# Keys and x transposed on VectorE and through DRAM instead of on TensorE

## The chip, the cores and the metric

The kernel runs on one core of a Trainium2 chip. The metric is the time of one execution in device microseconds; 0.3% of it is about 1 us. TensorE, VectorE, ScalarE, GpSimd and SyncE are five engines that run their own instruction streams in order and wait for each other by semaphores. In the profile they are PE (matmuls), PEld (weight loads of TensorE), DVE, ACT, POOL and SP; SP issues nearly all DMAs here.

## The reference

The first part is linear attention with a forget gate, for batch B = 4, H = 8 heads, S = 768 steps and head size D = 48. The second takes its output as x (4 x 768 x 384) through a rotation by learned angles, a mixing over steps with two 768x768 matrices, and a channel layer.

```python
f = 1.0 / (1.0 + np.exp(-f_logit))
for t in range(S):
    state = f[:, :, t, :, None] * state + np.einsum('bhd,bhe->bhde', k[:, :, t], v[:, :, t])
    y[:, :, t] = np.einsum('bhd,bhde->bhe', q[:, :, t], state)
# x: y with the heads side by side
theta = x @ w_theta
zr, zi = x * np.cos(theta), x * np.sin(theta)
y = np.einsum('ts,bsd->btd', w_tok_r, zr) + np.einsum('ts,bsd->btd', w_tok_i, zi)
u = x + y
return u + np.maximum(u @ w_ch, 0.0)
```

## The kernel before

A chunk is 128 steps of one batch with all heads; there are 24, six per batch. q, k and f of a chunk lie as [128, 4, 128]: two heads (each padded from 48 to 64 rows) fill the 128 partitions, four pairs stand side by side, and the 128 steps run along the row. The recurrence is turned into matrix products inside a chunk: the gates' logarithms are summed along the steps ("gs"), q is scaled by the running product p ("gq"), k by its inverse ("gk").

Everything after the set-up is written as a list of short steps, ORDER. The loop at its end (L578) takes one name after another, counts how often each name has come, and emits that step's instructions for that chunk, so the n-th "sc" is chunk n-1. A name with "/A", "/D" or "/P" is put on ScalarE, VectorE or GpSimd in place of its usual engine. No planner moves anything: each engine carries out its instructions in the order of the list, and so does SyncE with its DMAs.

For the attention of one chunk: "lf", "lk", "lq", "lv" load f, k, q and v; "go", "gs", "ge", "gp" make the gates; "ke" transposes the four key pairs on TensorE into PSUM (L321) and "kt" copies them to SBUF (L146 is the copy helper's line), because the state's update needs the steps on the partitions. "sc" (L295, L301) multiplies keys by v and keys by q; "ma" masks, "sa", "st", "sm" carry the state on, "oa" (L354) and "ob" (L365) multiply with state and v, "xc" copies the result to x, with steps on the partitions.

For the second part: "xt" transposes x in three blocks on TensorE (L377); from PSUM "xs" copies it to the u tile and "xh" and "xl" split it into a rounded value and the rest. "th" (L407) multiplies nine times by w_theta for the angles, "tn", "se", "ab", "tr" reduce them and take sine and cosine, "ro" multiplies by x, "zh" and "zl" split the result. 144 pieces "f" (L461) of six matmuls (the first 18 of two in full precision, four records each) add up the mixing; a group of 18 pieces is done for a batch and half of the steps. Then "v" adds to u, "uh" and "ul" split, "c" (L479, nine matmuls) is the channel layer, "cv" adds and "so" stores. "lw" loads weights, "d2" to "d5", "e4" and "e5" decode and split them; "wu" is a warm-up matmul. "fl" reduces a flag that says whether a rarely needed general branch must follow, "rv" loads it into registers, "bh" hints that branch.

Buffers: three each of f, k and q, two of v, one of transposed keys ("ktok"), three of x, three of u, one each of the rounded x and its rest, 25 of "wp" (values, weights and the first products' inputs), four PSUM banks "a" and four "mix".

Of the kernel before, what the change touches and what calls it, by code (L numbers as in the profile page):

```python
# [21 lines left out]
DM = H * D  # L22
# [23 lines left out]
CUT = 0  # L46

# [41 lines left out]
)  # L89


@with_exitstack
def gla_moe_kernel(
    ctx: ExitStack,
    tc: tile.TileContext,
    q: bass.AP,
    k: bass.AP,
    f: bass.AP,
# [286 lines left out]
    def u_slice(m):  # L385
        return uts[m // 3][:, :, m % 3 * C:(m % 3 + 1) * C]
# [318 lines left out]
```

## Time and profile before

| | |
|---|---|
| time, three runs | 334.07, 334.29, 334.9 us (median 334.29) |
| span of the profiled execution, first to last instruction | 331.3 us (its own time is not listed apart from the runs) |
| TensorE matmuls busy | 319.2 us, 4430 records |
| VectorE busy | 247.8 us, 448 instructions |
| ScalarE busy | 197.4 us |
| GpSimd busy | 49.3 us |
| DMA moved | 43.17 MB in 21,649 packets |
| granted TensorE clock | 0.999 of 2.4 GHz |

A matmul's length contains the time in which the next one already runs, so a busy TensorE may be less than a full one; the chain of waits has the pace at which groups follow each other. Full-precision matmuls have two records each.

### The profile page before, as it was taken

The numbers are of one execution on the slowest core, as the hardware profiler recorded it, in microseconds if no ns is written. First come the engines' busy times: TensorE is split into PE (matmuls) and PEld (weight loads), VectorE is DVE, ScalarE is ACT, GpSimd is POOL, SyncE is SP. The second block draws the span as 40 slices with busy tenths as digits, with TensorE's granted clock in tenths as the row PEclk, the third lists the DMA queues.
The fourth block names the chain that finished last, engine by engine and source line by source line (L and its number), as shares of the span: only waits on it lengthen the run. The fifth ranks groups of instructions, "written<-read, shape, count | busy, mean of one in ns | idle before, by whom it ended". The sixth has DMA issues, their size and how long they took to land.

```text
span 331.3 us, 10287 instructions
## 1 busy us (share of the span) xinstructions
PE 319.2 (96%) x4430; PEld 295.2 (89%) x4430; DVE 247.8 (75%) x448; ACT 197.4 (60%) x356; POOL 49.3 (15%) x65
## 2 busy tenths in 40 slices
PE   7689999999998999999999999999999999999993
PEld 7578677669998999999999999999999999999993
DVE  3789999999998999898954686766687868533252
ACT  6789999996888888574765378435844114300000
POOL 3230123124133310012101120200010100000000
PEclk9999999999999999999999999999999999999999
DMA  7979998567543270262126134108101000000022
GB/s 227 382 239 344 325 321 313 159 207 230 184 146 101 49 256 0 67 224 82 53 83 213 34 123 156 40 2 264 48 2 39 28 24 26 0 24 26 24 72 78
DMA packets 21649, 43.17 MB, mean 130 GB/s; under 512 B 2400, under 2 KB 5472, under 8 KB 21600
## 3 DMA queue, kind: packets, MB, share of 16 engines
q1 hardware_dynamic: 21456, 42.27, 38.4%
q8 instruction: 36, 0.59, 0.7%
q10 hardware_dynamic: 144, 0.20, 0.2%
q14 instruction: 13, 0.11, 0.1%
HBM read 37.74 MB, written 4.72 MB: 128 GB/s over the span
## 4 chain that ended last, share of the span: by engine, by line
PE 86%; DVE 5%; ACT 2%; DMA 2%; issue 1%; SPq 1%; DVEq 0%; ACTq 0%
PE pm L461 44%; PE pch L479 12%; PE pth L407 11%; PE pss L365 4%; PE pss L354 4%; PE pss L295 4%; PE pss L301 3%; PE psk L321 3%; PE pxt L377 2%; DMA v<-in_v_dram 2%; SPq L524 1%; DVE k L262 1%; ACT z L146 1%; DVE f L242 1%; PE warm L316 1%
## 5 line engine op out<-in xcount | busy, mean ns | idle before, releaser
L461 PE MATMUL pm<-wp,z 128*128 128x384 f32 x756 | 144.7, 340 | 0.0
L461 PEld LDWEIGHTS pm<-wp,z 128*128 128x128 f32 x756 | 130.3, 188 | 1.1 <-DVE wp L216 0.3
L479 PE MATMUL pch<-uhl,wch 128*128 128x384 f32 x216 | 41.4, 340 | 0.0
L479 PEld LDWEIGHTS pch<-uhl,wch 128*128 128x128 f32 x216 | 37.2, 188 | 0.2
L242 DVE TENSOR_TENSOR_SCAN f<-carry,f 128x512 f32<-128x512 f32 x24 | 29.1, 1217 | 5.0 <-ACT f L238 4.8
L407 PE MATMUL pth<-wth,xh 128*128 128x384 f32 x144 | 30.1, 344 | 0.9 <-ACT x L146 0.9
L146 ACT CAST uhl<-ut 128x384 fp32r<-128x384 f32 x12 | 6.2, 516 | 38.1 <-DVE uhl L146 19.9
L493 DVE SCALAR_TENSOR_TENSOR ut<-pch,ut 128x384 f32<-128x384 f32 x24 | 13.1, 554 | 20.7 <-PE pch L479 20.6
L407 PEld LDWEIGHTS pth<-wth,xh 128*128 128x128 f32 x144 | 24.7, 188 | 1.6 <-ACT x L146 1.2
L461 PE MATMUL pm<-value,zf 128*128 128x384 f32 x72 | 26.0, 497 | 0.0
L307 DVE TENSOR_TENSOR sc<-pss,causal 128x256 f32<-128x256 f32 x48 | 18.0, 416 | 8.4 <-PE pss L354 8.4
L257 POOL TENSOR_TENSOR q<-q,p 128x512 f32<-128x512 f32 x13 | 17.2, 1323 | 40.7 <-ACT p L249 39.3
L340 POOL TENSOR_TENSOR st<-st,pes 128x192 f32<-128x192 f32 x12 | 8.7, 721 | 95.9 <-DVE st L336 95.9
L249 ACT ACTIVATE p<-f 128x512 f32<-128x512 f32 x24 | 15.1, 628 | 9.8 <-DVE f L242 9.0
L253 POOL COPY pes<-p 128x4 f32<-128x4 f32 x24 | 11.4, 475 | 62.4 <-ACT p L249 62.4
L438 DVE TENSOR_TENSOR w<-w,x 128x768 f32<-128x768 f32 x18 | 17.4, 969 | 3.0 <-ACT w L431 2.9
L146 ACT COPY x<-pss 128x192 f32<-128x192 f32 x34 | 9.1, 318 | 17.1 <-PE pss L365 16.8
L262 DVE SCALAR_TENSOR_TENSOR k<-f,k 128x512 f32<-128x512 f32 x24 | 18.3, 763 | 1.2 <-ACT f L250 1.2
L461 PEld LDWEIGHTS pm<-value,zf 128*128 128x128 f32 x72 | 12.8, 189 | 7.0 <-DVE zf L438 0.4
L365 PEld LDWEIGHTS pss<-v,sc 64*64 64x64 f32 x768 | 15.7, 134 | 3.3 <-DVE w L438 0.8
L365 PE MATMUL pss<-v,sc 64*64 64x48 f32 x768 | 18.4, 222 | 0.1
L445 DVE TENSOR_TENSOR z<-w,z 128x768 fp32r<-128x768 f32 x18 | 17.1, 950 | 0.9 <-ACT z L146 0.9
(86 smaller groups left out, 570.7 us busy)
## 6 DMA issues: line engine op xcount, KB each, us to landing
v<-in_v_dram SPq DMA_DIRECT2D x24, 288.0 KB, 3.7
f<-in_f_dram SPq DMA_DIRECT2D x24, 256.0 KB, 3.6
q<-in_q_dram SPq DMA_DIRECT2D x24, 256.0 KB, 4.5
k<-in_k_dram SPq DMA_DIRECT2D x24, 256.0 KB, 4.1
raw<-in_w_r_dram SPq DMA_DIRECT2D x12, 383.8 KB, 4.9
raw<-in_w_i_dram SPq DMA_DIRECT2D x12, 383.8 KB, 5.5
out_dram<-ut SPq DMA_DIRECT2D x23, 192.0 KB, 2.1
raw<-in_w_theta_dram SPq DMA_DIRECT2D x3, 383.8 KB, 6.5
```

What stands on the lines that cost most here:

```text
L146: (nc.scalar.copy if on(usual) is nc.scalar else on(usual).tensor_copy)(dst, src)
L242: nc.vector.tensor_tensor_scan(fl, carry[:, pairs(h)].rearrange("p n t -> p (n t)"), fl, 0.0, ALU.mult, ALU.add)
L249: nc.scalar.activation(ps_[m][:, pairs(h)], ft, AF.Exp, scale=-1.0)
L257: on(nc.vector).tensor_tensor(qt, qt, ps_[m][:, pairs(h)], op=ALU.mult)
L262: nc.vector.scalar_tensor_tensor(kt, loaded["f", m][:, pairs(h)], E_TOP, kt, op0=ALU.min, op1=ALU.mult)
L307: masked = nc.vector.tensor_tensor(scs[m][j], pss[m][j][:, :, :64], causal.unsqueeze(1).to_broadcast([P, NP, 64]), op=ALU.mult)
L365: nc.tensor.matmul(pys[m][j][ts, p, :], l, r, start=(old[t] is None and p == 0), stop=(p == NP - 1))
L407: nc.tensor.matmul(pths[m], l, r, start=(n == 0), stop=(n == len(ms) - 1))
L438: nc.vector.tensor_tensor(zfs[m] if full else w, w, xs[m].unsqueeze(1).to_broadcast([P, 2, DM]), op=ALU.mult)
L445: nc.vector.tensor_tensor(zs[m][:, 0], zfs.get(m, ws.get(m)), zs[m][:, 1], op=ALU.subtract)
L461: nc.tensor.matmul(pms[g, d], l, r, start=(s == 0 and i == 0), stop=(s == NC - 1 and i == len(ms) - 1))
L479: nc.tensor.matmul(pcs[g, d], l, r, start=(es[0] == 0 and n == 0), stop=(es[-1] == KD - 1 and n == len(ms) - 1))
```

## The change

From chunk 12 on (the 13th), "ke" and "kt" are replaced by "kb", "ks", "kl". "kb" transposes the scaled keys on VectorE in 32x32 blocks inside each group of 32 partitions; "ks" writes the result to DRAM in four DMAs, one per 32 partitions, whose addresses put each block into its place, with rows of 32 values; "kl" loads the placed tile, rows of 128 values, into the one "ktok" buffer. In the same way "xb", "xw", "xr" replace "xt" and "xs": the load goes straight into the u tile, and "xh" and "xl" read it there. The buffer of the first weight decoder becomes the one buffer of transposed keys; x32 tiles use a "wp" buffer. The order of all steps is a new list, with engine marks of its own; the counts of all other steps stay. "fl", "rv" and "bh" stand earlier in it. A step may carry a chunk number after "@", which this list does not use.

```diff
--- before.py
+++ after.py
@@ -44,6 +44,8 @@
 FULL = 1
 
 CUT = 0
+KB, XB = 12, 12
+BL = 32
 
 
 
@@ -51,41 +53,42 @@
 
 
 ORDER = (
-    "wu wu wu wu wu lf wu go lf lf lq lk gs wu go ge go lk wu wu wu lw wu wu wu wu wu wu wu gs gq wu gp gk",
...
-    "ul e5/P ob e4 f xc ro zl e5 v f ge v f sa th d5 tn se ke kt zh c lf ab/A lf st gk cv tr sm d4 c d5/P",
-    "oa ma sc lv sa ob oa so d5 c ro ke v d4/D xt cv xc cv xh gp uh f ma f lq kt xl ob th xt so gs so zl lq",
-    "xh/D uh tn/D lk zh xc f se go xl gq/P lk go uh/D lv d5/P xt ge f xs/D ul f ab/A th gk xh zl f lk ul gq",
-    "tn xl se lf ke tr ab tr ul f f th ro gs c zh/D xs lf zl sc c cv ro xs tn/D lv sa zh f kt/D lk se st ge",
...
+    "lf lf wu lf wu lk wu lq wu lw wu wu lv wu go lk wu wu lq wu wu go gs wu lv wu wu wu ge gs wu wu gp",
...
+    "cv tn gk ro lf c se zh kb sc uh st ks zl go sm/P oa cv f gq/P sa ab/A ma so lq oa ul d5/P ob cv lq",
+    "tr so f ma so xc/D lk ob gs xt f ge ro gp f gq xh zh gk f xc xl lf d4 kb bh lv xt th kl zl ge d5/P",
+    "ks xs/D uh xh/D f tn go se lv xt xl gp th ul go xs/D gs f ab/A tn/D xs f gq xh se f ul xl c tr gk ab",
+    "lf ro tr sc kb kl cv th lk zh/D ks ro go c zl sa tn st ge f zh/D sm gp se f zl ab oa tr sc ma gs ob",
+    "f lv xc gk kl lq ro f so lk cv f kb so lf zh/D c xb zl xw f sa gs gq/P f cv so f v ks ge st uh/D f",
+    "ul gp v sm/P oa v uh sc go lq ma xr gk ob lk uh/D lf f xc ul lv xb f ul xw gq f sa xh st f kl ge xl",
+    "kb gp c gs ks sm/P th gk xr f lf tn go se oa sc lq ma ab/A cv ob lk gs c lv xc kl sa kb go f xb ks",
+    "gq/P cv f st sm/P ge f xw gp f xh gk lf oa sc tr ma kl kb ob lq sa c st xr ro lk ks gs xc f xl oa sm",
+    "gq/P xb th go f xh/D xw tn cv ge se f gp zh/D ab/A gk f so xl so so ma th lv tr zl lf lq kb f tn/D",
+    "se f ab xr ro f ks zh/D sc v ob gq/P lk f lv xc uh xb xh f sa xw v xl th zl ge uh/D kl gp f gk v f",
+    "kb tr uh/D oa ul tn ul f lq ul ks ma f ro c se lf zh xr ab gq/P tr ob cv sc ro lv xc kl f xb sa xw",
+    "zl go c xh/D st zh sm/P lk f so oa sc lq ma kl gs ob xr lk f sa ge cv f xl so gs lv xc th gq st xb c",
+    "sm/P tn xw xh se gp xl ab/A th zl cv gk so f tr kb tn f ro ks se f zh ab/A zl sc tr oa lk sa xr f ma",
+    "ro ge kl f lq st gp zh/D sm/P ob zl oa xc f xh xb gk xw f kb gq/P f xl lq f ks v uh th xr lv f tn se",
+    "f v ab/A v uh f ul go uh/D ul f ma xh ul f xl gs ob tr sc lv xc xb c sa ge th cv gq/P so gk xw f gp",
+    "tn se f ro ab/A kl f zh c xr tr f cv st kb f sm/P ks c xh so f cv ro f oa sc ma zl ob f lv xc/D so",
+    "sa xb f st xw xl sm/P f zh/D fl f kl zl rv th f xr tn/D se f v uh oa v sc ma xh uh/D ob sa ul oa xc",
+    "ab f tr ma xb xl th xw v ro uh f tn ul zh ul ob c xc/D se f cv xb c xw f cv xr ab zl f so tr f ro xr",
+    "c so xh xl f zh/D zl th xh f tn/D se f ab xl tr th f tn/D ro f cv zh se f so zl ab/A f tr f ro zh f",
+    "zl f f f v uh f v ul uh f v uh f f f f f f v ul uh f ul f f f f f f c f cv v so f f f c v ul c cv so",
+    "c uh uh/D ul ul c cv so c cv cv so cv so so",
 )
 
 
@@ -162,7 +165,7 @@
     raws, values = {}, {}
     SPLIT = [*range(NTOK), *range(NTOK + NC, NCH), *range(NTOK, NTOK + NC)]
 
-    tops = [const.tile([P, 2, TH], I32, tag="top0", name="top0"),
+    tops = [sb.tile([P, 2, TH], I32, tag="t32", bufs=1, name="top0"),
             sb.tile([P, 2, TH], I32, tag="uhl", bufs=4, name="top1")]
     for top in tops:
         nc.gpsimd.memset(top, 0)
@@ -324,6 +327,26 @@
         kts[m] = sb.tile([P, NP, P], F32, tag="ktok", bufs=1, name=f"ktok{m}")
         copy(nc.scalar, kts[m], psks[m])
 
+    NB = P // BL
+    k32s, kds = {}, {}
+
+    def keys_turn(n):
+        m = KB + n
+        k32s[m] = sb.tile([P, NP * P], F32, tag="t32", bufs=1, name=f"kt32{m}")
+        nc.vector.transpose(k32s[m], loaded["k", m].rearrange("q p t -> q (p t)"))
+
+    def keys_store(n):
+        m = KB + n
+        kds[m] = dram.tile([NP, P, P], F32, tag=f"kd{m}", name=f"kd{m}")
+        for a in range(NB):
+            nc.sync.dma_start(kds[m].rearrange("p (b t) d -> t (p b) d", b=NB)[:, :, a * BL:(a + 1) * BL],
+                              k32s[m][a * BL:(a + 1) * BL].rearrange("q (c i) -> q c i", i=BL))
+
+    def keys_load(n):
+        m = KB + n
+        kts[m] = sb.tile([P, NP, P], F32, tag="ktok", bufs=1, name=f"ktok{m}")
+        nc.sync.dma_start(kts[m], kds[m].rearrange("p t d -> t p d"))
+
     def att_mid(m):
         mids[m] = sb.tile([P, NP, D], F32, tag="sd", bufs=2, name=f"mid{m}")
         if m % NC == 0:
@@ -389,6 +412,27 @@
         if m % 3 == 0:
             uts[m // 3] = u_tile(m // 3)
         copy(nc.scalar, u_slice(m), pxts[m])
+
+    x32s, xds = {}, {}
+
+    def x_turn(n):
+        m = XB + n
+        x32s[m] = sb.tile([P, DM], F32, tag="wp", bufs=25, name=f"xs32{m}")
+        nc.vector.transpose(x32s[m], xs[m])
+
+    def x_store(n):
+        m = XB + n
+        xds[m] = dram.tile([KD, P, P], F32, tag=f"xd{m}", name=f"xd{m}")
+        for a in range(P // BL):
+            nc.sync.dma_start(xds[m].rearrange("k (r d) t -> d (k r) t", d=BL)[:, :, a * BL:(a + 1) * BL],
+                              x32s[m][a * BL:(a + 1) * BL].rearrange("q (c i) -> q c i", i=BL))
+
+    def x_load(n):
+        m = XB + n
+        if m % 3 == 0:
+            uts[m // 3] = u_tile(m // 3)
+        nc.sync.dma_start(u_slice(m), xds[m].rearrange("k d t -> d k t"))
+        pxts[m] = u_slice(m)
 
     def split_xh(m, src):
         xhs[m] = sb.tile([P, KD, P], F32R, tag="xh", bufs=1, name=f"xh{m}")
@@ -560,6 +604,8 @@
         "e4": lambda n: split_hi(NCH + n), "e5": lambda n: split_lo(NCH + n),
         "wu": warm_up, "gp": gate_end, "sa": att_mid,
         "sc": att_scores, "ma": att_mask, "ke": att_keys, "kt": att_ktok,
+        "xb": x_turn, "xw": x_store, "xr": x_load,
+        "kb": keys_turn, "ks": keys_store, "kl": keys_load,
         "st": inner(att_new), "sm": inner(att_fade), "oa": att_old, "ob": att_own, "xc": att_x, "xt": att_turn, "xs": keep_x,
         "xh": lambda m: split_xh(m, pxts[m]), "xl": lambda m: split_xl(m, pxts[m]),
         "th": angles, "tn": whole, "se": settle, "ab": fold, "tr": trig,
@@ -577,7 +623,9 @@
     done, engines = {}, {"": None, "A": nc.scalar, "D": nc.vector, "P": nc.gpsimd}
     for step in " ".join(ORDER).split():
         step, _, e = step.partition("/")
-        m = done[step] = done.get(step, -1) + 1
+        step, _, at = step.partition("@")
+        done[step] = done.get(step, -1) + 1
+        m = int(at or done[step])
         here[0] = engines[e]
         fn[step](m)
     here[0] = None
```

## Rows read from the trace of the kernel before

**Rows 1.** The page, busy time by engine: us, share, instructions.
```profile
PE 319.2 (96%) x4430; PEld 295.2 (89%) x4430; DVE 247.8 (75%) x448; ACT 197.4 (60%) x356; POOL 49.3 (15%) x65
```

**Rows 2.** The page, 40 slices of the span, busy tenths.
```profile
PE   7689999999998999999999999999999999999993
...
DVE  3789999999998999898954686766687868533252
...
PEclk9999999999999999999999999999999999999999
DMA  7979998567543270262126134108101000000022
```

**Rows 3.** Chain that ended last, by engine; then TensorE's longest wait, 20 to 326 us.
```profile
PE 86%; DVE 5%; ACT 2%; DMA 2%; issue 1%; SPq 1%; DVEq 0%; ACTq 0%
...
PE pth L407 <- ACT x L146: 0.9, 1, 0.9
```

**Rows 4.** Windows: length, busy PE, PEld, DVE, ACT, POOL, clock, DMA share, GB/s.
```profile
0.00:20.00 20.00, 14.58 (x296) 13.22 (x297) 12.03 (x23) 14.59 (x29) 7.15 (x17) 1.00 0.84 290
20.00:120.00 100.00, 98.24 (x1617) 82.34 (x1616) 96.96 (x163) 88.62 (x162) 26.55 (x24) 1.00 0.65 219
120.00:155.00 35.00, 35.00 (x479) 33.53 (x479) 32.02 (x58) 23.11 (x40) 3.59 (x7) 1.00 0.38 121
155.00:270.00 115.00, 115.00 (x1719) 110.37 (x1718) 79.45 (x154) 62.27 (x112) 11.97 (x17) 1.00 0.26 80
```

**Rows 5.** Pieces of the chain in order of time: start us, us, what.
```profile
28.45 0.59 PE psk L321 x4
...
200.37 0.48 PE pxt L377 x3
200.85 2.09 PE pm L461 x12
...
205.27 1.57 PE pth L407 x9
...
218.51 0.61 PE pss L295 x32
```

**Rows 6.** Groups by shape: busy us, mean ns, then idle before.
```profile
L242 DVE TENSOR_TENSOR_SCAN f<-carry,f 128x512 f32<-128x512 f32 x24 | 29.1, 1217 | 5.0 <-ACT f L238 4.8
...
L257 DVE TENSOR_TENSOR q<-q,p 128x512 f32<-128x512 f32 x11 | 7.7, 698 | 0.3 <-DMA q<-in_q_dram 0.3
...
L146 DVE COPY ktok<-psk 128x512 f32<-128x512 f32 x9 | 6.1, 682 | 1.9 <-PE psk L321 1.9
...
L146 DVE COPY ut<-pxt 128x384 f32<-128x384 f32 x8 | 4.4, 547 | 1.6 <-ACT xh L146 1.6
...
L146 DVE CAST uhl<-ut 128x384 fp32r<-128x384 f32 x12 | 4.2, 353 | 5.3 <-PE pch L479 5.3
```

**Rows 7.** DMA queues in the stretch 290 to 320 us: packets, MB, share; issues.
```profile
q1 hardware_dynamic: 576, 0.79, 7.3%
...
out_dram<-ut SPq DMA_DIRECT2D x5, 192.0 KB, 1.9
```

**Rows 8.** Tiles in_k_dram, then out_dram: issue ns min/median/max, and time to landing.
```profile
L524 SPq DMA_DIRECT2D k<-in_k_dram x24: 327/423/439, 2.8 to 226.6; - x24
...
DMA to landing us min/median/max: 2.6/4.1/6.7
...
DMA to landing us min/median/max: 1.8/2.1/6.0
```

**Rows 9.** Timeline near the end: start us, us, engine, operation.
```profile
325.34 1.60 DVE L493 SCALAR_TENSOR_TENSOR ut<-pch,ut 128x384 f32<-128x384 f32 x3 [2.09 <-PE pch L479]
```

44 rows, old and new, of the table ORDER are left out of this document.

## The prediction

> **What bounds the kernel now.** I read the page's busy line first [rows 1]: over a span of 331.3 us TensorE's matmuls are busy 319.2 us, VectorE 247.8 us, ScalarE 197.4 us. The 40 slices [rows 2] show that TensorE is full from the fourth slice to the last but one at the full granted clock, that VectorE is just as full up to about the twentieth slice and at 20 to 80% after it, and that the DMA engines are far from full after the first quarter. A full matmul row may still be waiting, so the chain of waits comes next [rows 3]: 86% of the span ends on TensorE, and after 20 us it waits by name for another engine only a little (the longest single wait, 0.9 us, is in rows 3). Cut into stages [rows 4], VectorE works 97.0 of the 100 us from 20 to 120 and 79.5 of the 115 us from 155 to 270. So TensorE's instruction stream sets the end, VectorE stands right beside it in the first half, and only in the second half is anything else free.
>
> **What is removed.** Twelve chunks lose four key transposes and three x transposes on TensorE. Matmuls overlap, so the length of one (about 270 ns) is no price; the chain gives the pace: four key transposes take 0.59 us, three x transposes 0.48 us, beside 2.09 us for twelve product matmuls (two pieces "f") and 1.57 us for the nine of "th" [rows 5]. So TensorE loses 12 x (0.59 + 0.48) = 12.8 us. All other matrix steps and the 28 warm-ups are as many as before. Twelve copies out of PSUM for keys and twelve for x go too, from ScalarE and VectorE together; VectorE's part by the marks in the two orders is five key copies of 0.68 us and four of x of 0.55 us [rows 6], 5.6 us in all.
>
> **What is added on VectorE.** Twelve transposes of 128x512 and twelve of 128x384. No row shows one. The quickest row of a pass from SBUF is the 128x384 cast at 0.35 us, 0.47 us for 512 columns; the slowest pass over 512 columns is the scan at 1.22 us, 0.91 us for 384 [rows 6]. I take the row of plain size and place, q times p, 0.70 us, and the x copy's 0.55 us: 12 x 1.25 = 15.0 us, against 5.6 us removed. Where this falls matters. I added up both orders step by step with the mean durations of the groups. At the place where 145 us of matrix steps are listed, the new order has listed 7 us more VectorE work than the old one: two more scans (2.4), four key transposes (2.8), two of x (1.1), three more "ul" (1.7), two "v" (1.1), against fewer conversions of weights (d4, minus 4.3) and fewer "tn" (minus 1.6), and smaller differences. Mean durations overlap by some 9%, so it is about 6.5 us. In the old run that place is reached at 155 us with VectorE busy 141.0 us [rows 4]; its idle 14.0 us were 8.0 in the first 20 us, 3.0 up to 120 us, 3.0 after. The start is built as before, so the first 8 us stay; if the 3 us up to 120 stay too and the last 3 go, VectorE is 141.0 + 6.5 + 11.0 = 158.5 us, 3.5 us late; if all later idle time goes, 0.5 us. I take 2.5 us, nearer to the first end, since 97% was the best that the old order reached. After this place VectorE falls behind TensorE's sum by 8 us within the next 30, and hides everything.
>
> **What is added in transfers.** Each of the 24 tiles goes out in four DMAs of 32 partitions and comes back in one. Stores have rows of 128 bytes: 12 x (2048 + 1536) = 43,008, or 2,688 per DMA engine. The nearest row is the stores of rows of 1,536 bytes: 7.3% of 16 engines over 30 us, 35 us in 576 packets, of which 512 carry data: 68 ns each [rows 7]. By bytes 128 would take 5.7 ns, by count 68 ns. Between them I take the mean in ratio, 20 ns: 54 us per engine. Loads add 672 rows of 512 bytes per engine, at 23 to 68 ns, for which I take 25 ns, 17 us. The old run has 0.38 x 35 + 0.26 x 115 = 43 us of DMA work from 120 to 270 us [rows 4]. 43 + 54 + 17 = 114 of about 150 us: full, but not the bound.
>
> The waits follow from the order. For every trip I summed the matrix time listed between its steps. From the transpose of x ("xb") to the step that needs it ("th") there are 9.8, 10.4 and 10.9 us for chunks 17, 21 and 23 (counted from 0) and 13.2 to 20.9 us for the other nine. The need: 0.55 transpose, 4 x 0.42 issues, 2.1 landing of a store, 0.42 issue, 4.1 landing of a load, 0.5 rounding [rows 8], 9.4 us. The keys' own trip is long (12.9 us or more), but its load ("kl") has one buffer and can only start when the chunk before has used it; from "kl" to "sc" stand 4.0, 4.3, 4.8, 4.8 and 5.5 us for chunks 19, 23, 15, 16 and 13 and 7.0 or more for the rest, where issue and landing need 4.5 us. v has 3.1 us for chunk 17 and 4.0 for 19. At median landings that is short by 1.4 + 0.5 + 0.2 = 2.1 us. At the longest landings of the rows (6.0 for a store, 6.7 for a load) x would be short by 25 us in all and keys by 12. I keep 0 and 37 us as ends and take 3 us, by the medians, since DMA is busier than before. All of this queues on SyncE, in order: "kl" and "xr" wait there for stores to land, and behind them stand the next loads of q, k, f and v and the output stores. q has only 2.6 to 5 us until it is scaled, but the scaling stands mostly on GpSimd and its reader 13 us or more behind it, so that delay is covered; f and k have 2.7 us or more and 4.7 us or more. The issues (96 + 24) x 0.42 = 50 us fit into SyncE's free time.
>
> **What costs nothing.** The flag's steps ("fl", "rv") and the branch hint come earlier; a short matmul of two records and a register load lie in other engines' shadow there. If they did not, VectorE would wait for TensorE at one place, up to the 7.5 us that it does today without delay. The first chunks' order changes all over, with the same counts on TensorE; the first 20 us are bounded by loads and gates as before. At the end stand, as before, the last three channel steps, three additions and the stores: the last addition begins to wait at 325.3 us and 5 to 6 us follow [rows 9]; I leave them.
>
> **The sum.** 331.3 - 12.8 + 2.5 + 3.0 = 324.0 us of span. The median of the runs is 334.3, which is 3.0 us above the profiled span; the profiled execution's own time is not listed, so I add these 3.0 us: **327.0 us**.
>
> **The rivals.**
> *All of it shows.* VectorE packs tighter and no landing is late: 331.3 - 12.8 + 3.0 = 321.5 us. For it: TensorE's waits are few today. Against it: the lockstep with VectorE.
> *VectorE's transposes are dear.* At the scan's pace six of them before the mark cost 4 x 0.52 + 2 x 0.36 = 2.8 us more, later ones hide: 329.8 us. For it: none is seen; against it: they are plain single-input passes. The Trainium skill, "VectorE: DVE Perf Modes", section "The three transpose paths", gives 311 ns for 128x128 of 16 bits; four and three of these would be an estimate of 1.24 and 0.93 us, the same case, and no row here bears it out.
> *Landings are a microsecond late.* If each landing, of store and of load, takes 1 us more than its median, x is short by 3.0, keys by 4.1 and v by 2.4 us: 9.5 in place of 3.0, 333.5 us, no gain. The need is met so narrowly that 1 us decides. For it: median landings of the rows come from DMA engines at a third of their time.
> *The DMA engines become the bound, and it is slower.* Place: between 120 and 270 us. Decisive: 150 - 43 - 17 = 90 us for 2,688 packets, 33 ns for a 128-byte row. At 45 ns, 32 us are added: 331.3 - 12.8 + 32 + 3.0 = 353.5 us; at 68 ns, 94 us, 415 us. Against it: 5.7 ns by bytes. For it: no row shows how short rows behave. The Trainium skill, "DMA: Bandwidth & Descriptors", section "Specifications", says that below 512 bytes a transfer is not at line rate because data is read, modified and written; were that a doubling, my 20 ns would be 40 ns and the time about 340 us. No stretch of this trace shows rows so short, so the rule carries the chance of this rival and not my forecast.
>
> **How the numbers follow.** The forecast (324 to 331 us) has 0.46, all of it 0.12, dear transposes 0.07, landings late (331 to 336 us) 0.15, DMA as the bound (above 336 us) 0.20. Two runs of this kernel can be told apart at about 0.3%, 1 us. Faster: 0.46 + 0.12 + 0.07 and half of the late landings, 0.72; same 0.05; slower 0.20 + 0.03 = 0.23. The range for 8 in 10 begins at the first rival, 321.5, and reaches to 340 us, into the last one; the likeliest case's own range is 324 to 331.
>
> **What would show it.** Right: 48 key and 36 x transposes left on TensorE and its busy time at about 307 us; VectorE's transposes at 0.55 to 0.75 us; VectorE above 95% from 20 to about 145 us; waits of "th" and "pss" for DMA few, for the short trips named. Wrong: a DMA share above 0.9 from 120 to 260 us, store landings of 5 us or more, or idle time of TensorE before each "sc" and "th".

## The result, and the profile after

The changed kernel takes 325.98 us (median of 4 runs, 324.9 to 329.21) beside 334.58 us for the kernel before (4 runs): a ratio of 0.9759 [0.9722, 0.9796], 8.6 us faster by the medians and 8.1 by the ratio; 327.0 was forecast. Ratios leave out disturbed executions and medians do not; where the two differ, both are given. The profiled execution took 325.77 us over a span of 324.0 us, so 1.8 us lie around the span. The forecast added 3.0.

The page of the changed kernel: busy time by engine, then the slices (one line each for TensorE, VectorE, its granted clock, DMA), then the chain by engine.

```profile
PE 312.3 (96%) x4346; PEld 288.6 (89%) x4346; DVE 245.7 (76%) x443; ACT 198.3 (61%) x357; POOL 49.6 (15%) x69
...
PE   7888999999999999999999999999999999999993
...
DVE  4889999899999998999657988787755686651041
...
PEclk9979999999999999999999999999999999999998
DMA  7989967957531568448887888956443414000012
...
PE 75%; DMA 8%; DVE 8%; issue 3%; SPq 2%; ACT 1%; POOL 1%; DVEq 0%; POOLq 0%; ACTq 0%
```

TensorE still looks full, but only 75% of the chain ends on it, against 86% [rows 3]; DMA has gone from 2% to 8% and VectorE from 5% to 8%. The DMA line, which fell away after the first quarter [rows 2], now stays at 0.5 to 0.9 through the middle. The windows say the same (length; busy PE, PEld, DVE, ACT, POOL with counts; clock; DMA share; GB/s):

```profile
0.00:20.00 20.00, 15.89 (x299) 14.73 (x299) 12.85 (x24) 14.21 (x28) 6.37 (x17) 0.95 0.86 311
20.00:120.00 100.00, 98.37 (x1614) 82.30 (x1610) 96.19 (x165) 91.99 (x165) 23.78 (x26) 0.99 0.65 214
120.00:155.00 35.00, 35.00 (x475) 34.00 (x474) 32.20 (x60) 23.90 (x45) 5.79 (x7) 1.00 0.68 180
145.00:185.00 40.00, 39.19 (x593) 37.34 (x592) 29.41 (x58) 20.95 (x40) 6.76 (x10) 1.00 0.81 205
```

VectorE packs from 20 to 120 us as before (96.2 against 97.0, [rows 4]). After the first 20 us the DMA share is highest in the row of 145 to 185 us, 0.81: high, not full. The groups that the change added on VectorE, and what it left on TensorE (busy us, mean ns, idle before):

```profile
L336 DVE STREAM_TRANSPOSE kt<-k 128x512 f32<-128x512 f32 x12 | 8.4, 703 | 0.1
L324 PE MATMUL psk<-ident,k 128*128 128x128 f32 x48 | 7.9, 290 | 0.7 <-ACT ut L149 0.7
L421 DVE STREAM_TRANSPOSE xs<-x 128x384 f32<-128x384 f32 x12 | 6.8, 568 | 1.3 <-ACT x L149 1.3
L400 PE MATMUL pxt<-ident,x 128*128 128x128 f32 x36 | 6.4, 288 | 0.8 <-DVE x L149 0.8
```

48 and 36 matmuls stay, and the transposes take 0.703 and 0.568 us where 0.70 and 0.55 were put.

**Where the time went.** A busy matmul row can be waiting, and TensorE's busy time fell by only 6.9 us, so starts are read instead. For each step take its start in the trace, less the sum of TensorE's steps listed ahead of it, each at a fixed pace: that is how far TensorE lags behind its own list. The pace of a step is how much later the next ones start because of it. In the trace of the kernel before, four key transposes and three x transposes, each followed by four pieces "f" and one more step (start, us, what):

```profile
180.92 0.60 PE L321 MATMUL psk<-ident,k 128*128 128x128 f32 x4
181.28 4.41 PE L461 MATMUL pm<-wp,z 128*128 128x384 f32 x24
185.52 1.73 PE L479 MATMUL pch<-uhl,wch 128*128 128x384 f32 x9
...
234.85 0.49 PE L377 MATMUL pxt<-ident,x 128*128 128x128 f32 x3
235.10 4.41 PE L461 MATMUL pm<-wp,z 128*128 128x384 f32 x24
239.35 1.20 PE L407 MATMUL pth<-wth,xh 128*128 128x384 f32 x6
```

From the first start to the last are 4.60 and 4.50 us. Four pieces "f" are 4.16 us of it (1.04 each, half of the 2.09 of [rows 5]); 0.44 us are left for the key transposes and 0.34 for those of x. A fit to the starts of all steps gives the same two paces within 0.03 us in both kernels. This is less than the 0.59 and 0.48 us of [rows 5], which stand right behind the attention's products. A piece of the chain runs from the end of one matmul to the end of the next, so behind those short matmuls (0.22 us each) it holds the passage to longer ones as well. That passage stays when the transposes go: in the trace of the kernel before, the step after "sc" starts 1.06 us behind it when it is "xt" and when it is "f".

So the lists differ by 12 x (0.44 + 0.34) = 9.4 us: 315.3 us before and 305.9 after (an estimate, with the other steps at paces from the same fit). The lag in us, as it grows between marks of listed work (up to 20 us it also holds the start; the last column is the whole lag at the last step):

| kernel (profiled execution) | up to 20 | 20 to 140 | 140 to 200 | 200 to 260 | at the end |
|---|---|---|---|---|---|
| before | 6.9 | 2.8 | 0.1 | 0.9 | 10.9 |
| after | 6.4 | 3.6 | 2.1 | 0.9 | 13.0 |

9.4 us less work and 2.1 us more lag make the 7.3 us by which the span fell from 331.3 to 324.0. Nearly all of the lag that is new lies between the marks 140 and 200, some 150 to 212 us in time. What SyncE did there in the changed kernel (start, us, DMAs of one kind in a row):

```profile
158.49 2.38 SPq L342 DMA_DIRECT2D kd<-kt  x4
...
161.47 0.50 SPq L568 DMA_DIRECT2D f<-in_f_dram  x1
...
163.65 2.39 SPq L348 DMA_DIRECT2D ktok<-kd  x1
166.09 2.53 SPq L342 DMA_DIRECT2D kd<-kt  x4
168.72 2.13 SPq L427 DMA_DIRECT2D xd<-xs  x4
170.94 1.78 SPq L568 DMA_DIRECT2D f<-in_f_dram  x1
...
173.33 0.49 SPq L568 DMA_DIRECT2D q<-in_q_dram  x1
```

And SyncE in the kernel before, in the same stretch of time:

```profile
163.75 0.39 SPq L524 DMA_DIRECT2D k<-in_k_dram  x1
164.18 0.42 SPq L524 DMA_DIRECT2D q<-in_q_dram  x1
164.70 0.38 SPq L524 DMA_DIRECT2D f<-in_f_dram  x1
173.71 0.33 SPq L529 DMA_DIRECT2D v<-in_v_dram  x1
```

Before, three loads and then 9 us of nothing. After, one issue follows close on another: from 145 to 185 us the records of 58 DMAs add up to 34.5 of 40 us (before: 15 and 6.2). Four stores take 2.1 to 2.5 us, and single loads of ktok and f stand 2.39 and 1.78 us where their like take 0.4. Over the whole run (issue ns, min/median/max):

```profile
L342 SPq DMA_DIRECT2D kd<-kt x48: 302/493/1798, 113.8 to 245.0; - x48
...
L427 SPq DMA_DIRECT2D xd<-xs x48: 303/474/2039, 145.1 to 269.4; - x48
```

So loads of q and f are issued late there. One piece of the chain of the changed kernel shows what becomes of it (start, us, what):

```profile
173.33 4.69 DMA q<-in_q_dram
...
178.15 1.30 POOL q L260
...
179.47 0.64 ACT p L252
...
180.14 0.64 ACT f L253
...
181.41 0.56 DVE xl L443
...
182.02 0.79 PE pth L451 x3
```

A late q holds GpSimd's scaling. That holds the only buffer p, so ScalarE's next gate waits; behind that stand VectorE's next steps, and with them the low half of x ("xl") that "th" reads. Here lies the largest single step of the lag in that stretch, 0.8 us. The longer waits of this path, summed over the changed kernel (us, times, longest):

```profile
POOL q L260 <- DMA q<-in_q_dram: 48.3, 7, 10.4
...
ACT p L252 <- POOL q L260: 10.1, 3, 5.7
```

In the kernel before:

```profile
POOL q L257 <- DMA q<-in_q_dram: 1.4, 1, 1.4
```

GpSimd's wait for q was 1.4 us before, and ScalarE's gate has no row of waiting for that scaling.

### The profile page after: what moved, and what is told of

The parts are those of the page before. It is cut to its first block, busy times and chain, and to the rows that moved or that the text cites. A ratio compares the mean times of both kernels' runs of the same rounds, so it can differ in the third digit from the quotient of the medians.

```text
span 324.0 us, 10330 instructions
## 1 busy us (share of the span) xinstructions
PE 312.3 (96%) x4346; PEld 288.6 (89%) x4346; DVE 245.7 (76%) x443; ACT 198.3 (61%) x357; POOL 49.6 (15%) x69
## 4 chain that ended last, share of the span: by engine, by line
PE 75%; DMA 8%; DVE 8%; issue 3%; SPq 2%; ACT 1%; POOL 1%; DVEq 0%; POOLq 0%; ACTq 0%
PE pm L505 40%; PE pch L523 10%; PE pth L451 9%; DMA q<-in_q_dram 4%; PE pss L388 3%; PE pss L377 3%; PE pss L298 3%; PE pss L304 3%; DMA v<-in_v_dram 2%; DMA raw<-in_w_i_dram 2%; PE psk L324 1%; PE pxt L400 1%; DVE sc L310 1%; SPq L568 1%; POOL q L260 1%
## 5 line engine op out<-in xcount | busy, mean ns | idle before, releaser
L505 PE MATMUL pm<-wp,z 128*128 128x384 f32 x756 | 141.7, 339 | 0.0
L149 ACT CAST uhl<-ut 128x384 fp32r<-128x384 f32 x17 | 8.6, 511 | 45.0 <-DVE ut L509 29.9
L537 DVE SCALAR_TENSOR_TENSOR ut<-pch,ut 128x384 f32<-128x384 f32 x24 | 13.1, 549 | 20.3 <-PE pch L523 20.3
L260 POOL TENSOR_TENSOR q<-q,p 128x512 f32<-128x512 f32 x13 | 16.8, 1291 | 69.7 <-DMA q<-in_q_dram 48.3
L509 DVE TENSOR_TENSOR ut<-pm,ut 128x384 f32<-128x384 f32 x24 | 13.1, 551 | 11.8 <-PE pm L505 11.8
L265 DVE SCALAR_TENSOR_TENSOR k<-f,k 128x512 f32<-128x512 f32 x24 | 16.9, 703 | 5.3 <-ACT f L253 5.2
L505 PEld LDWEIGHTS pm<-value,zf 128*128 128x128 f32 x72 | 12.8, 190 | 6.8
L256 POOL COPY pes<-p 128x4 f32<-128x4 f32 x24 | 8.5, 353 | 62.6 <-ACT p L252 62.6
L474 ACT ACTIVATE w<-w 128x384 f32<-128x384 f32 x24 | 12.6, 524 | 8.6 <-DVE w L469 8.2
```

Of the source, the lines that this page charges most:

```text
L260: on(nc.vector).tensor_tensor(qt, qt, ps_[m][:, pairs(h)], op=ALU.mult)
L265: nc.vector.scalar_tensor_tensor(kt, loaded["f", m][:, pairs(h)], E_TOP, kt, op0=ALU.min, op1=ALU.mult)
L505: nc.tensor.matmul(pms[g, d], l, r, start=(s == 0 and i == 0), stop=(s == NC - 1 and i == len(ms) - 1))
L509: nc.vector.tensor_tensor(u, pms[g, d], u, op=ALU.add)
```

## The experiments

All are the changed kernel but for the edit shown, unless the text says otherwise; times are medians, ratios stand against the kernel before on the same chip.

**1. The order alone.** All 24 chunks transpose on TensorE again, in the new order; "ke kt" stand up to eight steps ahead of "sc", "xt xs" just ahead of "xh". (A first list, with the transposes at the places of the loads, gave no time: its steps wait for each other in a circle.)

```diff
- kb ... ks ... kl ... sc        (twelve chunks)
+ ke kt ... sc
- xb ... xw ... xr ... xh        (twelve chunks)
+ xt xs xh                       (four of them with "xh xl" moved as well)
```

> The new order with the 24 tiles transposed on TensorE again: key transposes and their copy stand up to eight steps ahead of sc, x transposes and copy just ahead of xh (for four chunks xh and xl moved with them). Theory: the gain is TensorE's 84 transposes, 12 x (0.59 + 0.44) = 12.3 us, less about 5 us of waits that the trips through DRAM and the closer packing brought. So this gives 326 + 12.3 - 2 to 4 (the waits of the trips go) = 334 to 336 us, the time of the kernel before. Rival: the new order by itself packs better and the transposes matter less; then 331 us or less.

Measured: 342.8 us, 1.0255 [1.0212, 1.0298]. Slower than the kernel before, where 334 to 336 was expected. Its waits, 120 to 300 us:

```profile
PEld pth L450 <- ACT xh L148: 5.2, 6, 1.2
...
PE pth L450 <- ACT xh L148: 3.8, 4, 0.9
```

"th" waits six times for the rounding of an x that stands just ahead of it in this list; transposed sooner, it would hold one of four PSUM banks for longer. With this placing the order gains nothing without the mechanism. How much the placing adds to that, and how much is the order's own, the run does not separate.

**2. The mechanism in the old order.** Nine of the late chunks send their keys through DRAM, the store where "ke" stood, the load where "kt" stood. (The whole mechanism does not fit into the old order, since a load would stand on SyncE ahead of what it waits for; this was not tried.)

```diff
- ke ... kt
+ kb ks ... kl                   (chunks 12, 14 to 19, 22, 23)
```

> The old order with the keys of nine chunks (12, 14 to 19, 22, 23) taken through VectorE and DRAM, x as before; transpose and stores stand where the TensorE transpose stood, the load where its copy stood. TensorE loses 9 x 0.59 = 5.3 us. Theory: a trip needs about 9.8 us (transpose 0.7, four issues 2.0, store landing 3.2, issue 0.4, load landing 3.5) and the old order gives 1.7 to 7.8 us of matrix time for eight of the nine, short by 35 us in all: net about 30 us slower than before, 360 us, TensorE idle ahead of sc. Rival: transfers are covered anyway by what TensorE has queued; then 329 us.

Measured: 362.58 us, 1.0848 [1.0814, 1.0883], as expected; the rival's 329 is out. Waits, 120 to 300 us:

```profile
PE pss L299 <- DMA ktok<-kd: 12.7, 3, 6.0
```

TensorE waits for the loads themselves; the granted clock is 0.91 from 145 to 185 us, between its two levels of 1.2 and 2.4 GHz, where it was 1.00 in the kernel before. So with 9 x 0.44 = 4.0 us less listed work the kernel is 28 us slower when the trips have no room. Room for the trips is a condition of the gain; that the new order is the only way to it was not tried.

**3. Only x through DRAM.** Keys return to TensorE.

```diff
- kb ... ks ... kl ... sc
+ ke kt ... sc
```

> The changed kernel with the keys of chunks 12 to 23 transposed and copied on TensorE and ScalarE again, up to eight steps ahead of sc; x still through DRAM. TensorE gets 12 x 0.59 = 7.1 us back; SyncE loses 60 of its 120 added DMAs, VectorE 8.4 us. Theory that SyncE and VectorE cost some 3 to 5 us in the change, half of it from the keys: 326 + 7.1 - 2 = 331 us. Rival: both kinds of trip cost nothing by themselves: 333 us.

Measured: 331.25 us, 0.9865 [0.9829, 0.9902], as expected. x alone gives 3.8 us by the medians (4.5 by the ratio), the keys the other 4.8 (3.6). At 0.44 us the list is 5.3 us longer than the change's, not 7.1, and the lag from 20 to 260 is 5.7 us (6.6 in the change): the keys' trips earn 5.3 and hand back 0.9. At this price the rival, trips that cost nothing by themselves, comes to 326 + 5.3 = 331.3 us too, so the run does not tell the two apart.

**4. Each transpose twice**, and **5. none** (the stores read k and x as they are, so the blocks come out untransposed). The edits are shown for k; x alike.

```diff
+        for _ in range(2):
             nc.vector.transpose(k32s[m], loaded["k", m].rearrange("q p t -> q (p t)"))
...
-        nc.vector.transpose(k32s[m], loaded["k", m].rearrange("q p t -> q (p t)"))
+        k32s[m] = loaded["k", m].rearrange("q p t -> q (p t)")
```

> The changed kernel with every VectorE transpose carried out twice: 15 us more on VectorE, of which 4 x 0.70 + 2 x 0.57 = 3.9 us lie before 155 us. Theory: VectorE is full up to 155 us and covered after: 3 to 4.5 us slower, 329 to 330.5 us. Rivals: all of it is covered, 326 us; or VectorE bounds the second half too and 10 us or more show.

> The changed kernel without VectorE's transposes; the stores read keys and x as they are (leaves out the transposes; 15 us of VectorE's 246 us; same DMAs). With every transpose doubled the time rose by 7.2 us. Theory that VectorE's time counts half wherever it is put, by the path from keys and x to the trip's end and by a full VectorE up to 155 us: 2 to 5 us faster. Rival: the doubled kernel met a limit that the single one does not reach: within 1 us of 326.

Measured: twice 333.17 us, 0.9953 [0.9929, 0.9977]; none 326.42 us, 0.9719 [0.967, 0.9767]. Doubling adds 15.6 us of transposes on VectorE and 7.2 us to the time (6.5 by the ratio), well above the 3 to 4.5 that was expected. Against the change, the lag grows by 2.0 us more between the marks 20 and 140, where six of the transposes stand, and by 4.0 more from 140 to 260. So VectorE does not hide everything in the second half. It was busy 61.2 of the 77 us from 185 to 262 with the doubling, so it is not simply full there; that a transpose stands at the head of a trip is the likely reason, not a shown one. Leaving all of it out gains 1.3 us by the ratio and nothing by the medians, inside the intervals, as the rival had it; the lag from 20 to 260 is 4.7 us in place of 6.6. One set of transposes costs little; a second of the same size is paid for by nearly half.

**6. Long rows.** The stores write rows of 2,048 and 1,536 bytes, contiguous, in place of 128; the blocks are not placed. (Shown for k; x alike, here and in 7.)

```diff
-  kds[m].rearrange("p (b t) d -> t (p b) d", b=NB)[:, :, a * BL:(a + 1) * BL], k32s[m][a * BL:(a + 1) * BL].rearrange("q (c i) -> q c i", i=BL)
+  kds[m].rearrange("p t d -> (p t d)").rearrange("(q c) -> q c", q=P)[a * BL:(a + 1) * BL], k32s[m][a * BL:(a + 1) * BL]
```

**7. The same in one store.** As 6, with one DMA of 128 partitions per tile: 72 DMAs fewer.

```diff
-  for a in range(NB): nc.sync.dma_start(...)
+  nc.sync.dma_start(kds[m].rearrange("p t d -> (p t d)").rearrange("(q c) -> q c", q=P), k32s[m])
```

> The changed kernel with the stores of transposed tiles in rows of 2,048 and 1,536 bytes, as they lie (leaves out the placing of blocks; same bytes, same number of DMAs, same loads and waits). Theory that the loss between 155 and 205 us (3.2 us of TensorE against its list) comes from DMA engines kept busy by 43,008 short rows, 36 us per engine, and from the longer issue of such stores: 1 to 3 us faster, 323 to 325 us. Rival: it comes from the fixed time of a trip and a landing, whatever the rows: within 0.5 us of 326.

> As e5_long_rows (transposed tiles stored as they lie, placing left out), but each tile in one DMA of 128 partitions in place of four of 32: 72 DMAs fewer on SyncE, the same bytes, transposes, loads and waits. Theory that SyncE, which issues back to back from 145 to 185 us, makes loads late there: against e5's 325.7 us 1 to 3 us faster, 323 to 324.5 us, and TensorE's loss against its list between the marks of 140 and 200 us of matrix steps falls from 1.9 us (e5) and 3.0 us (the change) to 1 us or less. Rival: landings and fixed times of the trip make that loss: within 0.5 us of e5.

Measured: long rows 325.7 us, 0.9734 [0.9702, 0.9765]; one store 324.37 us, 0.9692 [0.9655, 0.9729]. The window 145 to 185 us, long rows first:

```profile
145.00:185.00 40.00, 40.00 (x601) 38.70 (x600) 32.11 (x63) 20.85 (x41) 6.76 (x10) 1.00 0.78 233
```

and one store:

```profile
145.00:185.00 40.00, 40.00 (x601) 38.70 (x601) 32.04 (x63) 20.74 (x40) 7.17 (x11) 1.00 0.76 243
```

Packets in this stretch fell from 20,501 to 8,148 with long rows, the DMA share from 0.81 to 0.78, and the time by 0.3 us (0.8 by the ratio, with overlapping intervals): nothing that can be told, as the rival had it. The short rows cost this kernel no time that these runs can show. With one store per tile SyncE's records there fall to 37 DMAs and 16.8 us, and SyncE has gaps again. The time is 1.3 us below that of long rows, as expected, but the intervals overlap. The lag from 140 to 200 is 0.6 us (0.8 with long rows, 2.1 in the change; the 1.9 and 3.0 of the expectation come from the dearer paces).

**8. Half of the stores from ScalarE**, **9. all from GpSimd**, **10. output stores from GpSimd** (all groups but the last).

```diff
-            nc.sync.dma_start(kds[m]...
+            (nc.scalar if a % 2 else nc.sync).dma_start(kds[m]...     (8, x alike)
+            nc.gpsimd.dma_start(kds[m]...                             (9, x alike)
...
-        queue = nc.scalar if g == B * NTH - 1 and d == 1 and not general else nc.sync
+        queue = nc.scalar if g == B * NTH - 1 and d == 1 and not general else nc.sync if general or g == B * NTH - 1 else nc.gpsimd
```

> The changed kernel with two of each tile's four stores issued from ScalarE instead of SyncE. Theory that SyncE's issue stream (about 2.5 to 3.5 us for the four stores of a tile, back to back from 150 to 185 us) makes the next q, f and v loads late: 1 to 2 us faster. Rival: landing time of the loads, not their issue, is what is late; then no change, or 1 to 3 us slower, because ScalarE now stands in line for VectorE's transposes.

> The changed kernel with all four stores of each tile issued from GpSimd, not SyncE. In the trace of the change SyncE issues DMAs for 34.5 of the 40 us from 145 to 185 us, with 0.5 us of waits and short gaps between: it is full, and TensorE loses 3 us against its list from 150 to 205 us. Theory that SyncE's issue stream makes loads late there: the loss shrinks, 1 to 3 us faster (323 to 325 us), if GpSimd's own issues are short. Rival: GpSimd needs more than 1 us to issue a store of 512 rows, and its q scalings and state fades come late: 3 us or more slower.

> The changed kernel with the output stores of all groups but the last issued from GpSimd, not SyncE (21 DMAs, of which 4 stand between 145 and 185 us). Theory that SyncE's queue is what is late: about 0.5 to 1.5 us faster. Rival: no change; or slower, since GpSimd then waits for the additions.

Measured: 328.85 us, 0.9825 [0.9795, 0.9856]; 331.06 us, 0.9867 [0.9835, 0.9898]; 328.28 us, 0.9803 [0.9753, 0.9853]. The first two are slower than the change (the intervals of the first just overlap), as the rivals had it, and the third gains nothing. SyncE is relieved in each (145 to 185 us: 20.3, 12.8 and 31.2 us of records against 34.5), but the issues land on an engine that also computes. GpSimd's groups in 9:

```profile
L342 POOL DMA_DIRECT2D kd<-kt x48 | 31.4, 662 | 22.9 <-DVE kt L336 16.3 <-DVE st L359 3.7 <-DVE uhl L149 2.2
L427 POOL DMA_DIRECT2D xd<-xs x48 | 29.5, 621 | 33.6 <-DVE xs L421 22.4 <-DVE st L359 5.3 <-DVE mid L353 3.1
```

61 us of issues on GpSimd, and before its stores it waits 38.7 us for VectorE's transposes, with q's scaling behind. The Trainium skill, "DMA: Bandwidth & Descriptors", section "Issuing engines are not separate DMA queues", says that starting DMAs from several engines saves only sequencer time, usually small beside the DMA itself. For one store that holds here, 0.49 us of issue (median) beside 3.2 us to landing; it is the sum in one stretch, 34.5 of 40 us, that is large. Moving it did not help, since an engine that works in order holds up what stands behind a store.

**11. Free the buffer p.** From chunk 12 on q is multiplied by zeros, not by p, so a late q holds no gate back (the scaling of q is left out).

```diff
-        on(nc.vector).tensor_tensor(qt, qt, ps_[m][:, pairs(h)], op=ALU.mult)
+        by = ps_[m][:, pairs(h)] if m < KB else carry[:, :, 0:1].to_broadcast([P, NP, C])
+        on(nc.vector).tensor_tensor(qt, qt, by, op=ALU.mult)
```

> The changed kernel where from chunk 12 on q is multiplied by zeros that are at hand, not by p (leaves out the scaling of q; same operation, same size), so that the single buffer of p is free before q has come. Theory: the waits of TensorE between 165 and 185 us (2.1 us) come from late q loads, through GpSimd's scaling, p's single buffer, ScalarE's next p and the keys: 1.5 to 2.5 us faster, ScalarE no longer waiting for GpSimd. Rival: they come from VectorE being full or from loads of x; then within 0.5 us.

Measured: 326.79 us, 0.9767 [0.9736, 0.9798]: no change. ScalarE's wait for GpSimd is gone, and other rows stand in its place (120 to 300 us):

```profile
POOL q L261 <- DMA q<-in_q_dram: 45.7, 7, 9.1
...
PEld pth L452 <- ACT xh L149: 1.1, 1, 1.1
```

The theory that this path sets the lag fell: it was the one that came last, and the next is as long (lag from 140 to 200: 2.1 us, as in the change).

**12. The flag's steps late again**: "fl" and "rv" near the end of the list.

```diff
- ... fl f kl zl rv th ...
+ ... fl f ... c rv ...
```

> The changed kernel with fl ahead of piece f139 and rv behind channel step 19, near the end as before. In the trace of the change TensorE loses 0.5 us at 252.5 us, where the small matmul of fl waits for VectorE's reduction. Theory: that 0.5 us comes back, 0.2 to 0.6 us faster. Rival: it only moves; same time.

Measured: 326.43 us, 0.9754 [0.971, 0.9798]. The 0.5 us by which "pf" waits in the trace is gone; the time shows nothing of it.

## Why the prediction was right, and which steps were not

The direction was forecast for the right reason, less work on a full TensorE. That the time came out so near is luck: the work removed and the waits were both put 3.4 us too high.

**The work removed** is the term that was most mis-sized: 12.8 us forecast, 9.4 by the starts. The forecast rightly did not take a matmul's length as its price, but the chain's pieces that it took, 0.59 and 0.48 us [rows 5], stand behind attention products and hold a passage that stays; the steps behind gain 0.44 and 0.34. The price of VectorE's transposes was right.

**The DMA engines** were costed too high and did not matter. The page's queue of the kernel before (packets, MB, share) and of the changed one:

```profile
q1 hardware_dynamic: 21456, 42.27, 38.4%
```

```profile
q1 hardware_dynamic: 77136, 53.29, 56.3%
```

0.563 x 324.0 less 0.384 x 331.3 is 55 us more for each DMA engine, where 54 + 17 = 71 was forecast. The trace's 128-byte packets take 13.2 ns in the mean, not 20, those of 512 bytes 28.6, not 25. The rival of a DMA bound needed 33 ns, and experiment 6 shows nothing measurable left of it. The Trainium skill's rule of 512 bytes ("DMA: Bandwidth & Descriptors", section "Specifications") says that less is not at line rate. The trace agrees: a 128-byte row of a store takes nearly half the time of a 512-byte row of a load. No run shows a step that this slows.

**VectorE's lockstep** was mis-sized: 2.5 us forecast, 0.3 by the whole lag up to mark 140 (0.8 between 20 and 140, less 0.5 before). That "VectorE falls behind TensorE's sum and hides everything" later failed too: experiment 4 took 4.0 us more there.

**The transfers' term** was 3.0 us; the lag after mark 140 is 2.0 us larger than before, 0.4 of it the flag's step that was costed at nothing. Two claims under it were wrong. That the issues "fit into SyncE's free time" was a sum over the run; in 145 to 185 us they fill it, a store at 0.47 to 0.49 us in the median, not 0.42. That q's delay "is covered" looked at q's reader alone and not at the buffer p that the scaling holds. But the landings were as forecast, and so the rival of late ones did not come (last column: median us from issue to landing):

```profile
kd<-kt SPq DMA_DIRECT2D x48, 64.0 KB, 3.2
ktok<-kd SPq DMA_DIRECT2D x12, 256.0 KB, 3.5
xd<-xs SPq DMA_DIRECT2D x48, 48.0 KB, 2.4
ut<-xd SPq DMA_DIRECT2D x12, 192.0 KB, 2.9
```

Store and load together are 6.7 us for a tile of keys and 5.3 for one of x, where 2.1 + 4.1 = 6.2 was put. Between 120 and 262 us no row of "th" or "pss" waits for DMA above 0.3 us; the rounding of x ("xh") waits 5.1 us in all for its loads, ahead of "th".

These errors cancel: 12.8 - 2.5 - 3.0 = 7.3 was forecast, and 9.4 - 2.1 = 7.3 came, with a span of 324.0 both times. **What lies around the span** was the last error. The difference of 3.0 us between the profiled span and the median was read as overhead; it is 1.8, and the profiled execution of before was some 1.5 us quicker than the median. Its granted clock was 0.999. Of the later executions of that kernel, those at 0.998 or 0.999 had spans of 331.4 to 332.1 us and most others, at 0.980 to 0.995, 332.1 to 335.2. The profiled execution of the change has lost some clock: it was at the lower of the two levels, 1.2 GHz, from 18.2 to 21.6 us (columns as in the windows above, the clock third from the end):

```profile
18.20:21.60 3.40, 3.40 (x44) 2.98 (x43) 2.89 (x7) 3.34 (x10) 0.65 (x2) 0.50 0.72 213
```

At half the clock these 3.4 us cost up to 1.7 us (an estimate). So the two spans are not quite like with like, which is one reason why 8.6 us by the medians stand beside 7.3; how much of the 2.1 us of lag is the clock's stays open.

**The busy time** of 307 us was a bad sign to name: it fell to 312.3, by 6.9 us, where 9.4 us of work went and 2.1 us of lag came, which a busy row can hold. Of the other signs, VectorE was busy 95.7% from 20 to 145 us, as said.

**What stays open** is what makes the 2 us between the marks 140 and 200. The lag there, beside SyncE's records from 145 to 185 us, in eight profiled executions:

| kernel | lag 140 to 200, us | DMAs | SyncE, us |
|---|---|---|---|
| before | 0.1 | 15 | 6.2 |
| only x (3) | 0.8 | 41 | 19.6 |
| one store (7) | 0.6 | 37 | 16.8 |
| long rows (6) | 0.8 | 64 | 27.0 |
| no transposes (5) | 1.2 | 59 | 32.4 |
| flag late (12) | 0.7 | 61 | 32.8 |
| p free (11) | 2.1 | 60 | 32.2 |
| after | 2.1 | 58 | 34.5 |

The two largest stand with a crowded SyncE, but so does experiment 12, whose list is the change's own up to there: 0.7 and 2.1 us are what two executions of the same steps differ by. So crowded issue on SyncE is not shown as the cause, and later landings are not excluded. No kernel that computes all of the reference was measurably quicker than the change; one store per tile is 2.2 us below it by the ratio, with intervals that just overlap, and does not place the blocks.

## What to carry to other kernels

Work taken off a full engine is worth the time by which it puts off the steps behind it, read from starts among steps of its own kind: neither its busy time nor its piece of the chain, which can hold a passage that stays. Part comes back as lag: find where by subtracting the listed work from each step's start, and distrust a lag that falls. When transfers are added, sum the issuing queue over the crowded stretch, not over the run, and follow a late load to every buffer that its consumer holds. A trip through DRAM needs room in the order first (without it nine trips cost 28 us here), and a wait at the end of the chain is worth nothing until the next path is looked at.

## What the runs showed of the hardware

- VectorE's 32x32 transpose runs like a plain pass: 703 ns for 128x512 of f32, beside 698 ns for the product of q and p [rows 6].
- A store row of 128 bytes took 13.2 ns of a DMA engine, far from the 68 ns of a 1,536-byte row; with rows 12 to 16 times longer the kernel's time stayed the same within the intervals.
- The same store costs its issuer 0.49 us on SyncE and 0.65 us on GpSimd (medians).
- Four f32 transposes of 128x128 through TensorE put off the next steps by 0.44 us and three by 0.34, some 0.11 us each, while the record of one is about 0.27 us long.
- Up to the mark of 20 us the lag was 5.0 to 8.7 us over twelve kernels whose steps are the same there. It goes with the granted clock: 5.0 to 6.1 us in the three executions that stayed at the upper level, 6.4 to 7.6 in the five with 3.4 us at the lower one (from 17 to 20 us on), 8.2 to 8.7 in the four with 6.8 us. What makes the clock fall in one execution and not in another no run shows. Part of the spread between runs (324.9 to 329.21 us) may arise there, but not all: the run of 329.21 us has the mean clock of the profiled one, 0.992. So differences under 0.5% stay open here.
